# Chunk 2's loads in one run and its transposes behind all of them: a retention recurrence with a SwiGLU network on one core

## The chip, the core and the metric

The kernel runs on one core of a Trainium2 chip. The metric is the device time of one execution in microseconds (us). Five engines have in-order instruction queues of their own: TensorE (PE in the profile; PEld is its weight load), VectorE (DVE), ScalarE (ACT), GpSimd (POOL) and SyncE (SP, which here only issues DMAs). They meet through semaphores. DMAs that POOL issues appear in the profile as software DMAs on queue q0, those that SP issues as hardware DMAs on q1; TensorE's instructions come in on q8.

## The reference

Inputs are q, k, v of shape (4, 8, 768, 64): batch B, heads H, positions S, head width D. Each head h has a decay, and a recurrence over positions; its output, all heads side by side, goes through an RMS norm and a gated feed-forward network.

```python
gamma = 1.0 - 2.0 ** (-5.0 - np.arange(H))
for t in range(S):
    state = gamma[None, :, None, None] * state + np.einsum('bhd,bhe->bhde', k[:, :, t], v[:, :, t])
    y[:, :, t] = (1 / np.sqrt(D)) * np.einsum('bhd,bhde->bhe', q[:, :, t], state)
x = y.transpose(0, 2, 1, 3).reshape(B * S, H * D)          # 3072 x 512
xn = x / np.sqrt(np.mean(x * x, axis=-1, keepdims=True) + 1e-06) * rms_g
g = xn @ w_gate                                            # 512 x 1536
out = (g * sigmoid(g) * (xn @ w_val)) @ w_out              # 1536 x 512
```

The output is 3072 x 512 in float32.

## The kernel before

**Chunks and groups.** The 768 positions are cut into six chunks of 128. Within a chunk the recurrence is a masked product of q and k, applied to v (which carries the decay), plus q times the state from the chunks before. A chunk of all four batches is 512 tokens. The feed-forward network of chunk c is called group c here: twelve blocks of 128 hidden units in `gv` (gate and value products, eight or more matmuls each, then Silu on ScalarE and the multiplication `hT` on VectorE), and then `down`, once for each batch. The work of the recurrence for chunk c + 1 is placed between the steps of group c, so that TensorE has group c to work on while the other engines prepare the next chunk.

**Two ways to get q and k transposed.** Chunks 0 and 1 come as pairs of batches (`load_pair`, tiles q2b, k2b, v2f) and are transposed by TensorE. From chunk 2 on, `load` (line 103) issues three loads for one batch on POOL's queue: q and k, converted to bfloat16 on the way (qb, kb), and v in float32 (v_f). `t_dma` (line 486) then issues two DMA transposes on SP's queue, qb to qT and kb to kT. `vp` (line 480) on POOL multiplies v by its decay.

**The recurrence from chunk 2 on.** `a_pair(c, p)` makes the q-k products of the two batches of pair p on TensorE (line 499, tile a_ps, two PSUM banks a batch). `a_mask` multiplies them with the causal mask on VectorE (line 508). `values(c, p)` (line 518) adds three products: qT with the state, k with vp for the state's new term (bank kv_ps), and the masked products with vp. Then `y_out` (VectorE), `square` (ScalarE), `rstd` (POOL), `norm` (VectorE, tile xn) and `x_dma` (a DMA transpose on SP, xn to xnT, line 554) bring the pair's 256 tokens into the form that the next group's `gv` reads. `state_add` (VectorE, line 550) adds kv_ps to the float32 state, `state_cast` (POOL) makes its bfloat16 copy.

**What sets the order.** There is no scheduler: every engine executes its instructions in the order in which the program's text issues them (`manual_schedule`). For groups 1 and later, `run(steps, after)` issues step i of the list `steps` and then what the table `after` lists under i. Group 1 has sixteen steps: 0 to 11 are `gv`, of which 0 to 5 take the first 256 tokens (pair 0) and 6 to 11 the other 256, and 12 to 15 are `down` of batches 0 to 3. An entry of the table thus stands behind its step's matmuls in TensorE's queue, and behind that step's `hT` in VectorE's queue.

**Buffers.** A tile of the pools has a fixed number of buffers (8 of qb, kb, qT and kT, 6 of v_f), and an instruction that writes a buffer waits for its last reader. From group 1 on, PSUM's eight banks are two rotations: banks 0 to 3 serve the recurrence, 4 to 7 the network:

```python
        if i is None and split[0]:
            i = turn[ffn] % 4 + 4 * ffn
            turn[ffn] += 1
```

In the rotation of group 1, `values(2, 0)` takes banks 2 and 3 for y_ps and 0 for kv_ps, and `a_pair(2, 1)`, the next to ask, takes 1 and 2 for its first batch and 3 and 0 for its second.

**Where chunks 2 and 3 are loaded.** Before, the loads of chunk 2 are spread over the end of group 0, a batch at a time, with the transposes of a batch soon after: t_dma(2, 0) stands in SP's queue between the stores of group 0, and t_dma(2, 1) behind down(0, 3). Chunk 3 is loaded in steps 3 to 9 of group 1 and transposed in steps 8 to 12.

Of the kernel before, what the change touches and what calls it, by code (L numbers as in the profile page):

```python
# [16 lines left out]
def kernel(  # L17
# [11 lines left out]
    nc = tc.nc  # L29
# [58 lines left out]
    U = {}  # L88

# [13 lines left out]
    def load(c, b, names="qkv"):  # L103
        u = U.setdefault((c, b), {})
        for n in names:
            if n == "v":
                x = work.tile([128, H, D], F32, name="v_f", tag="v_f", bufs=6)
                nc.gpsimd.dma_start(out=x, in_=unit_v[n][c, b])  # L108
            else:
                x = work.tile([128, DM], BF16, name=n + "b", bufs=8)  # L110
                nc.gpsimd.dma_start(out=x.rearrange("p (h d) -> p h d", h=H), in_=unit_v[n][c, b])  # L111
            u[n] = x

# [372 lines left out]
    def t_dma(c, b):  # L486
        u = U[c, b]
        for n in "qk":
            t = work.tile([128, NHP, 128], BF16, name=n + "T", tag=n + "T", bufs=8)
            nc.sync.dma_start_transpose(out=t, in_=u[n])  # L490
# [98 lines left out]
    def down(c, b, n0=0, n1=NFF):  # L589
# [4 lines left out]
        if n1 == NFF:  # L594
            o_sb = work.tile([128, DM], F32, name="o_sb", bufs=3)
            nc.scalar.copy(o_sb, DP[b])  # L596
            store(nc.sync, c, b, slice(0, DM), o_sb)

# [103 lines left out]
    for n in "qk":  # L702
        load_pair(1, 1, n)
    vp_pair(1, 0)
    load_pair(1, 1, "v")
    load(2, 0)
# [25 lines left out]
    norm1(0)  # L732
    load(2, 1)
    vp_pair(1, 1)
    load(2, 2)
    t_dma(2, 0)
# [9 lines left out]
    load(2, 3)  # L746
    t_dma(2, 1)
    down(0, 3, 4, NFF)
    ap(1, 1, 0)
# [6 lines left out]
    def run(steps, after):  # L756
        for i, step in enumerate(steps):
            step()
# [3 lines left out]
    def L(f, *a):  # L762
# [8 lines left out]
        2: [L(begin, 2), L(norm, 1, 1, 0, 1), L(state_cast, 1), L(vp, 2, 0), L(vp, 2, 1), L(t_dma, 2, 2),  # L771
            L(t_dma, 2, 3)],
        3: [L(load, 3, 0)],
        4: [L(x_pe, 1, 1, 0), L(x_copy, 1, 1, 0, "v"), L(x_pe, 1, 1, 1), L(x_copy, 1, 1, 1, "a"), L(load, 3, 1)],
        5: [L(a_pair, 2, 0), L(a_mask, 2, 0, 0)],
        6: [L(a_mask, 2, 0, 1), L(a_mask, 2, 1, 0), L(vp, 2, 2), L(vp, 2, 3)],
        7: [L(a_mask, 2, 1, 1)],
        8: [L(values, 2, 0), L(load, 3, 2), L(t_dma, 3, 0), L(t_dma, 3, 1)],
        9: [L(y_out, 2, 0, 0), L(y_out, 2, 0, 1), L(state_add, 2, 0), L(load, 3, 3)],
        10: [L(a_pair, 2, 1), L(square, 2, 0, 0), L(a_mask, 2, 2, 0), L(a_mask, 2, 2, 1), L(state_cast, 0)],  # L780
        11: [L(square, 2, 0, 1), L(rstd, 2, 0), L(a_mask, 2, 3, 0), L(a_mask, 2, 3, 1), L(t_dma, 3, 2)],
        12: [L(values, 2, 1), L(norm, 2, 0, 0, 1), L(x_dma, 2, 0, 0), L(x_dma, 2, 0, 1), L(t_dma, 3, 3),
# [64 lines left out]
```

## Time and profile before

| | before |
|---|---|
| median of 13 runs | 245.06 us |
| lowest, highest run | 240.59, 249.2 us |
| profiled execution, its own time | 243.45 us |
| its span, first to last instruction | 241.5 us |
| mean granted TensorE clock | 0.985 |
| TensorE busy | 230.2 us, 95% of the span |
| POOL busy | 118.4 us, 49% |
| software DMA queue q0 | 52544 packets, 17.04 MB |
| hardware DMA queue q1 | 30224 packets, 12.72 MB |
| landing of a load of v_f, median of 16 | 8.2 us after its issue |
| landing of a kT transpose, median of 16 (least 2.4, most 10.2) | 7.2 us after its issue |

A DMA's row in a timeline is the time that the issuing engine spends on issuing it; when its data have landed is told apart, in the DMA view. In the busy rows a digit is the busy share of a fortieth of the span, in tenths. An idle time in square brackets is that of the engine just before the instruction, with what ended it; "issue" means that the profile shows nothing that it waited for. The clock column is the share of full speed that TensorE was granted. The DMA share sums the time of packets that overlap, so it can be above 1.

### The profile page before, as it was taken

Reading aid. Unit: us, or ns where it says so; the run is one execution under the profiler, and the core shown is the slowest. Engines: PE = TensorE matmul, PEld = TensorE weight load, DVE = VectorE, ACT = ScalarE, POOL = GpSimd, SP = SyncE. Lnnn points to the kernel's source line nnn. Section 1 sums busy time; section 2 is a strip of 40 time slices with the busy share of each in tenths; the row PEclk is TensorE's granted clock in tenths of the full one; section 3 lists DMA queues with packets and bytes.
Section 4 is the critical chain, followed back from the end, with each engine's and each line's share of the span. In section 5 each row is a group of like instructions: output and inputs, shape, how many; then the busy total and the mean of one; then the engine's idle time right before and its main releaser. Section 6 shows DMA issues by size and latency. Waiting matters only on the chain.

```text
span 241.5 us, 5543 instructions
## 1 busy us (share of the span) xinstructions
PE 230.2 (95%) x2281; PEld 138.3 (57%) x2281; DVE 127.5 (53%) x219; ACT 88.6 (37%) x178; POOL 118.4 (49%) x154
## 2 busy tenths in 40 slices
PE   7897999999889999999999999999999999999993
PEld 2465774455678875586454585454684444864443
DVE  3867433356756677826866437866245842234300
ACT  2866434208243243235323225313225242333221
POOL 8992948887959951990955901937001001000000
PEclk9978899999999999999999999999999999999999
DMA  9999999999999999999697993999520304200022
GB/s 109 157 175 190 160 172 148 177 205 167 142 197 155 155 184 128 189 145 204 49 153 173 115 169 131 101 121 174 134 86 0 46 0 124 96 0 0 0 90 87
DMA packets 83467, 30.25 MB, mean 125 GB/s; under 512 B 71602, under 2 KB 79026, under 8 KB 83443
## 3 DMA queue, kind: packets, MB, share of 16 engines
q0 software_dynamic: 52544, 17.04, 71.5%
q1 hardware_dynamic: 30224, 12.72, 29.0%
q8 instruction: 18, 0.29, 0.5%
q10 hardware_dynamic: 674, 0.14, 0.3%
q14 instruction: 7, 0.05, 0.1%
HBM read 28.32 MB, written 6.29 MB: 143 GB/s over the span
## 4 chain that ended last, share of the span: by engine, by line
PE 75%; DMA 7%; DVE 6%; POOL 5%; issue 3%; SPq 2%; ACT 1%; POOLq 0%; DVEq 0%; ACTq 0%
PE g_ps L571 23%; PE v_ps L571 23%; PE o_ps L593 20%; DMA v2f<-in_v_dram 3%; DMA kT<-kb 2%; DMA xnT<-xn 2%; DVE xn L468 2%; DVE am L508 2%; PE a_ps L499 1%; PE y_ps L544 1%; DVE hT L576 1%; SPq L490 1%; POOL q2b L99 1%; POOL k2b L99 1%; PE o_ps L605 1%
## 5 line engine op out<-in xcount | busy, mean ns | idle before, releaser
L576 DVE TENSOR_TENSOR hT<-sg,v_ps 128x512 bf16<-128x512 bf16 (+1 forms) x75 | 49.7, 664 | 76.1 <-PE v_ps L571 72.1
L571 PE MATMUL g_ps<-xnT,wg_b 128*128 128x256 bf16 (+1 forms) x424 | 75.5, 312 | 2.4 <-issue 1.9
L571 PE MATMUL v_ps<-xnT,wv_b 128*128 128x256 bf16 (+1 forms) x424 | 75.6, 313 | 0.0
L575 ACT ACTIVATE sg<-g_ps 128x512 bf16<-128x512 f32 (+1 forms) x75 | 43.4, 580 | 85.4 <-PE g_ps L571 85.4
L593 PE MATMUL o_ps<-wo_b,hT 128*128 128x512 bf16 x276 | 62.1, 379 | 0.1
L571 PEld LDWEIGHTS <-wv_b 128*128 128x128 bf16 x424 | 41.8, 99 | 21.4
L571 PEld LDWEIGHTS <-wg_b 128*128 128x128 bf16 x424 | 40.2, 98 | 23.0 <-issue 2.9
L593 PEld LDWEIGHTS <-hT 128*128 128x128 bf16 x276 | 26.4, 98 | 31.2 <-issue 0.4
L460 POOL TENSOR_SCALAR m<-ms 128x2 f32<-128x2 f32 x10 | 2.2, 219 | 69.3 <-ACT xsq L455 69.3
L596 ACT COPY o_sb<-o_ps 128x512 f32<-128x512 f32 x23 | 13.2, 580 | 33.8 <-PE o_ps L593 33.8
L468 DVE SCALAR_TENSOR_TENSOR xn<-x,rstd,g_bc 128x512 bf16<-128x512 f32 x18 | 18.5, 1054 | 8.5 <-POOL rstd L375 8.5
L508 DVE TENSOR_TENSOR am<-a_ps,causal 128x512 bf16<-128x512 f32 x32 | 20.8, 680 | 0.0
L482 POOL TENSOR_TENSOR vp<-v_f,vd_n 128x512 bf16<-128x512 f32 x16 | 20.1, 1278 | 0.0
L455 ACT ACTIVATE xsq<-x 128x512 bf16<-128x512 f32 x20 | 12.4, 623 | 13.5 <-DVE x L446 7.7
L111 POOL DMA_DIRECT2D qb<-in_q_dram x16 | 15.1, 942 | 0.0
L108 POOL DMA_DIRECT2D v_f<-in_v_dram x16 | 14.8, 924 | 0.0
L111 POOL DMA_DIRECT2D kb<-in_k_dram x16 | 14.4, 901 | 0.0
L220 PE MATMUL hot<-ones 128*128 128x512 bf16 x27 | 10.4, 521 | 1.4 <-DVE ones L143 1.4
L446 DVE TENSOR_TENSOR x<-y_ps,yd_n 128x512 f32<-128x512 f32 x16 | 10.8, 684 | 0.6 <-PE y_ps L544 0.6
L305 POOL TENSOR_TENSOR vp<-v2f,vd_p 128x1024 bf16<-128x1024 f32 x4 | 7.6, 1928 | 0.6 <-DMA v2f<-in_v_dram 0.6
L375 POOL TENSOR_TENSOR rstd<-m,mhalf 128x2 f32<-128x2 f32 x10 | 7.2, 718 | 0.8
L288 DVE TENSOR_TENSOR am<-a_ps,causal_p 128x512 bf16<-128x512 f32 x8 | 5.0, 684 | 2.6 <-PE a_ps L281 2.6
(99 smaller groups left out, 162.2 us busy)
## 6 DMA issues: line engine op xcount, KB each, us to landing
v_f<-in_v_dram POOLq DMA_DIRECT2D x16, 256.0 KB, 8.2
out_dram<-o_sb SPq DMA_DIRECT2D x15, 256.0 KB, 2.2
out_dram<-o_sb SPq DMA_DIRECT2D x17, 128.0 KB, 5.6
qb<-in_q_dram POOLq DMA_DIRECT2D x16, 128.0 KB, 6.5
kb<-in_k_dram POOLq DMA_DIRECT2D x16, 128.0 KB, 6.9
v2f<-in_v_dram POOLq DMA_DIRECT2D x7, 256.0 KB, 6.1
wo_b<-in_moe_w_out_dram POOLq DMA_DIRECT2D x3, 512.0 KB, 7.1
wg_b<-in_moe_w_gate_dram POOLq DMA_DIRECT2D x5, 256.0 KB, 6.7
```

The costliest lines, as they stand in the source:

```text
L108: nc.gpsimd.dma_start(out=x, in_=unit_v[n][c, b])
L111: nc.gpsimd.dma_start(out=x.rearrange("p (h d) -> p h d", h=H), in_=unit_v[n][c, b])
L446: nc.vector.tensor_tensor(out=x[:, :, :, i, :], in0=u["y"][i].rearrange("p (b a d) -> p b a d", b=2, a=NHP), in1=yd_n[:, c, i][:, None, :, ...
L455: nc.scalar.activation(xsq, u["x"][:, b], AF.Square, scale=1.0 / math.sqrt(DM), accum_out=u["ms_"][:, b:b + 1])
L468: nc.vector.scalar_tensor_tensor(out=u["xn"][b], in0=u["x"][:, b], scalar=u["rstd"][:, b:b + 1], in1=g_bc, op0=ALU.mult, op1=ALU.mult)
L482: nc.gpsimd.tensor_tensor(out=x, in0=U[c, b]["v"], in1=vd_n[:, c, :, None].to_broadcast([128, H, D]), op=ALU.mult)
L508: nc.vector.tensor_tensor(out=x, in0=u["a_ps"][i].rearrange("p (a t) -> p a t", a=NHP), in1=causal[:, None, :].to_broadcast([128, NHP, 128 ...
L571: nc.tensor.matmul(x[:, o:o + w], wt[:, s, n * 128:(n + 1) * 128], XT[c][:, s, t0:t1], start=s == 0, stop=s == KS - 1)
L575: nc.scalar.activation(sg[:, :m], ps[0][:, :m], AF.Silu)
L576: return nc.vector.tensor_tensor(out=HT[c][:, n0:n1, t0:t1], in0=sg[:, :m].rearrange("p (n t) -> p n t", t=w), in1=ps[1][:, :m].rearrange( ...
L593: nc.tensor.matmul(DP[b], HT[c][:, n, b * C:(b + 1) * C], wo_b[:, n, :], start=n == 0, stop=n == NFF - 1)
L596: nc.scalar.copy(o_sb, DP[b])
```

## The change

It has four parts.

1. The loads. v of pair (1, 1) is loaded ahead of its q and k, and POOL's product of it (`vp_pair(1, 1)`) comes up directly behind. q and k of batch (2, 0) are loaded where they were, and its v joins the run of loads of batches 1, 2 and 3, which POOL now issues with nothing between them.
2. The transposes of chunk 2. All eight are issued in one place, behind down(0, 3) and all stores of group 0 in SP's queue, and each waits for the last load of chunk 2 (`t_dma(2, b, "load")`, v of batch 3).
3. Chunk 3. Its first load waits for the `hT` of step 8 of group 1, and that of batch 2 for the o_sb copy of step 13 (`down` of batch 1), so that the loads of each half begin no earlier; the transposes of batches 0 and 1 come in step 10, those of 2 and 3 in step 15.
4. The recurrence in group 1. a_pair(2, 0) moves from step 5 to 7, values(2, 0) from 8 to 10, a_pair(2, 1) from 10 to 11, values(2, 1) from 12 to 13, a_pair(3, 0) from 14 to 15. state_add(2, 0) goes from behind y_out in step 9 to behind a_pair(2, 1) and the first of its masks in step 11.

The number of instructions on each engine, and what they compute, stay the same.

```diff
-    def load(c, b, names="qkv"):
+    def load(c, b, names="qkv", after=None):
...
+            if after is not None and after in MARK:
+                tc.add_manual_dep(i.ins, MARK[after].ins.name, SYNC_DEP, reason="transfer order")
             u[n] = x
+            MARK["load"] = i
...
-    def t_dma(c, b):
+    def t_dma(c, b, after=None):
...
-            nc.sync.dma_start_transpose(out=t, in_=u[n])
+            i = nc.sync.dma_start_transpose(out=t, in_=u[n])
+            if after is not None:
+                tc.add_manual_dep(i.ins, MARK[after].ins.name, SYNC_DEP, reason="transfer order")
...
-    for n in "qk":
-        load_pair(1, 1, n)
+    load_pair(1, 1, "v")
+    load_pair(1, 1, "q")
     vp_pair(1, 0)
-    load_pair(1, 1, "v")
-    load(2, 0)
+    load_pair(1, 1, "k")
+    load(2, 0, "qk")
+    vp_pair(1, 1)
...
     norm1(0)
+    load(2, 0, "v")
     load(2, 1)
-    vp_pair(1, 1)
     load(2, 2)
-    t_dma(2, 0)
+    load(2, 3)
...
-    load(2, 3)
-    t_dma(2, 1)
     down(0, 3, 4, NFF)
+    for b in range(B):
+        t_dma(2, b, "load")
...
-            step()
+            MARK[i] = step()
...
-        2: [L(begin, 2), L(norm, 1, 1, 0, 1), L(state_cast, 1), L(vp, 2, 0), L(vp, 2, 1), L(t_dma, 2, 2),
-            L(t_dma, 2, 3)],
-        3: [L(load, 3, 0)],
-        4: [L(x_pe, 1, 1, 0), L(x_copy, 1, 1, 0, "v"), L(x_pe, 1, 1, 1), L(x_copy, 1, 1, 1, "a"), L(load, 3, 1)],
-        5: [L(a_pair, 2, 0), L(a_mask, 2, 0, 0)],
-        6: [L(a_mask, 2, 0, 1), L(a_mask, 2, 1, 0), L(vp, 2, 2), L(vp, 2, 3)],
-        7: [L(a_mask, 2, 1, 1)],
-        8: [L(values, 2, 0), L(load, 3, 2), L(t_dma, 3, 0), L(t_dma, 3, 1)],
-        9: [L(y_out, 2, 0, 0), L(y_out, 2, 0, 1), L(state_add, 2, 0), L(load, 3, 3)],
-        10: [L(a_pair, 2, 1), L(square, 2, 0, 0), L(a_mask, 2, 2, 0), L(a_mask, 2, 2, 1), L(state_cast, 0)],
-        11: [L(square, 2, 0, 1), L(rstd, 2, 0), L(a_mask, 2, 3, 0), L(a_mask, 2, 3, 1), L(t_dma, 3, 2)],
-        12: [L(values, 2, 1), L(norm, 2, 0, 0, 1), L(x_dma, 2, 0, 0), L(x_dma, 2, 0, 1), L(t_dma, 3, 3),
-             L(y_out, 2, 1, 0), L(y_out, 2, 1, 1), L(state_add, 2, 1), L(square, 2, 1, 0), L(square, 2, 1, 1),
-             L(rstd, 2, 1), L(norm, 2, 1, 0, 1), L(x_dma, 2, 1, 0), L(x_dma, 2, 1, 1),
-             L(state_cast, 1), L(vp, 3, 0), L(vp, 3, 1)],
-        14: [L(a_pair, 3, 0), L(a_mask, 3, 0, 0, 1), L(a_mask, 3, 1, 0, 1)],
+        2: [L(begin, 2), L(norm, 1, 1, 0, 1), L(state_cast, 1), L(vp, 2, 0), L(vp, 2, 1)],
+        4: [L(x_pe, 1, 1, 0), L(x_copy, 1, 1, 0, "v"), L(x_pe, 1, 1, 1), L(x_copy, 1, 1, 1, "a")],
+        5: [L(vp, 2, 2), L(vp, 2, 3)],
+        7: [L(a_pair, 2, 0), L(a_mask, 2, 0, 0)],
+        8: [L(a_mask, 2, 0, 1), L(a_mask, 2, 1, 0), L(load, 3, 0, "qkv", 8)],
+        9: [L(a_mask, 2, 1, 1), L(load, 3, 1)],
+        10: [L(values, 2, 0), L(y_out, 2, 0, 0), L(y_out, 2, 0, 1), L(t_dma, 3, 0), L(t_dma, 3, 1)],
+        11: [L(a_pair, 2, 1), L(square, 2, 0, 0), L(square, 2, 0, 1), L(rstd, 2, 0), L(a_mask, 2, 2, 0),
+             L(state_add, 2, 0), L(state_cast, 0)],
+        12: [L(a_mask, 2, 2, 1), L(norm, 2, 0, 0, 1), L(x_dma, 2, 0, 0), L(x_dma, 2, 0, 1), L(a_mask, 2, 3, 0),
+             L(a_mask, 2, 3, 1)],
+        13: [L(values, 2, 1), L(load, 3, 2, "qkv", 13), L(y_out, 2, 1, 0), L(y_out, 2, 1, 1), L(square, 2, 1, 0),
+             L(square, 2, 1, 1), L(rstd, 2, 1), L(state_add, 2, 1), L(load, 3, 3), L(norm, 2, 1, 0, 1),
+             L(x_dma, 2, 1, 0), L(x_dma, 2, 1, 1), L(state_cast, 1), L(vp, 3, 0), L(vp, 3, 1)],
+        15: [L(a_pair, 3, 0), L(a_mask, 3, 0, 0, 1), L(a_mask, 3, 1, 0, 1), L(t_dma, 3, 2), L(t_dma, 3, 3)],
```

## The prediction

> **What bounds the kernel now.** I read the page first, then the busy time by stretches, then the timelines of TensorE, SP, POOL and VectorE from 40 us to 145 us, and last the DMA view in narrow windows, which gives one transfer's time from issue to landing.
>
> ```profile
> PE 230.2 (95%) x2281; PEld 138.3 (57%) x2281; DVE 127.5 (53%) x219; ACT 88.6 (37%) x178; POOL 118.4 (49%) x154
> ...
> DMA  9999999999999999999697993999520304200022
> ```
>
> TensorE is busy for 230.2 of 241.5 us, so all idle time that any change can remove is 11.3 us, and the kernel's start and its final tail hold most of it. The DMA row shows that the 16 engines are busy for the whole first half, where chunk 2 is fetched. The table by stretches (fields: stretch, length, then each engine's busy time, granted clock, DMA share, GB/s) finds what is left:
>
> ```profile
> 61.00:74.00 13.00, 11.05 (x189) 9.60 (x182) 9.12 (x14) 4.70 (x10) 10.57 (x12) 1.00 1.94 180
> 74.00:89.00 15.00, 14.65 (x192) 12.34 (x190) 9.92 (x17) 4.89 (x9) 13.50 (x16) 1.00 1.87 151
> 89.00:107.20 18.20, 18.01 (x201) 10.91 (x198) 11.83 (x17) 5.97 (x13) 11.44 (x14) 1.00 1.46 153
> ```
>
> From 61 to 107 us, the stretch of group 1, TensorE idles 1.95 + 0.35 + 0.19 us. That 2.5 us is the most the change can win there in this execution. The DMA share of 1.94 and 1.87 (packet time summed over overlapping packets) marks where loads and transposes share the engines. TensorE's timeline names the gaps:
>
> ```profile
> 64.65 0.83 PE L571 MATMUL g_ps<-xnT,wg_b 128*128 128x256 bf16 x6
> 67.43 0.39 PE L571 MATMUL g_ps<-xnT,wg_b 128*128 128x256 bf16 x2 [1.95 <-issue]
> ...
> 76.06 0.62 PE L499 MATMUL a_ps<-qT,kT 64*128 64x128 bf16 x16
> ...
> 87.70 0.38 PE L499 MATMUL a_ps<-qT,kT 64*128 64x128 bf16 x7 [0.33 <-DVE st_f L550]
> ...
> 107.21 1.05 PE L571 MATMUL g_ps<-xnT,wg_b 128*128 128x256 bf16 x8 [0.20 <-DMA xnT<-xn]
> ```
>
> The 1.95 us gap waits for no semaphore. In 64 to 67 us the DMA view has one packet of 0.02 MB on the instruction queue (q8), and the bandwidth falls to 0 to 14 GB/s for over a microsecond, so I read it as TensorE out of instructions behind a clogged DMA system (argued, not shown). The product of the first pair (76.06) does not wait for its transposes: the last of them, kT of batch 1, was issued at 65.04 and landed after 9.4 us, at 74.4. The SP queue and the DMA view give the transfers:
>
> ```profile
> 74.72 1.19 SPq L490 DMA_TRANSPOSE qT<-qb  x1
> 78.01 1.19 SPq L490 DMA_TRANSPOSE kT<-kb  x1
> ```
>
> ```profile
> 66.46 0.95 POOL L108 DMA_DIRECT2D v_f<-in_v_dram  x1
> ```
>
> ```profile
> v_f<-in_v_dram POOLq DMA_DIRECT2D x1, 256.0 KB, 12.2
> ```
>
> ```profile
> kT<-kb SPq DMA_TRANSPOSE x1, 9.4
> ```
>
> ```profile
> kT<-kb SPq DMA_TRANSPOSE x1, 2.4
> ```
>
> The last load of chunk 2 was issued at 66.46 and took 12.2 us, to 78.7. A transpose among loads takes 9.4 us; the same transpose alone (issued at 132.17) takes 2.4 us and SP issues one each 1.3 us (130.87, 132.17, 133.47).
>
> **What the Trainium skill says.** "DMA: Bandwidth & Descriptors", section "Issuing engines are not separate DMA queues": DMAs from POOL and SP run on the same 16 engines and interleave. The 9.4 against 2.4 us agree. The same page, section "Two DMAs through the same engine are not ordered", says that order needs a wait of the issuing engine on the earlier DMA's semaphore; that is what the change adds on SP, so everything behind it in SP's queue waits too. "TensorE: Matmul & The Clock Gate", section "What's actually happening": the clock halves after about one idle window of 3.4 us. The trace agrees in part: after 19.40 to 22.81 (1.74 us busy) the clock is 0.50 until 26.22, but after 63.77 to 67.18 (1.71 us busy) it stays 1.00. No page prices an instruction fetch that comes late.
>
> **The change part by part.** Times are on the clock of the profiled execution.
>
> *Loads.* v of (1,1) goes ahead of its q and k, its 1.94 us product on POOL (60.19) moves to about 52.6, into POOL's idle 2.4 us before 55.94, and v of (2,0) moves from 52.6 to 57.5. From 57.5 POOL then issues ten loads of chunk 2 at 0.91 us each (median of the rows), to 66.6: no gain on POOL. k of (1,1) is now issued at 49.4 to 50.8; v in that slot landed at 55.6 and 57.1, and its transposes start at 57.9. Cover 0.8 us, cost nothing; if it fails, a few tenths.
> When does the last load land? Without transposes beside them, six loads issued from 103.03 to 107.51 landed from 106.9 (3.9 us) to 114.4 (6.9 us): 1.5 us each, stores among them. The first here is issued at 57.5 and lands after 4.0 us as before, at 61.5; nine more at 1.45 us: **74.5**. From below: POOL's last issue 65.7 plus 3.4 us (the quickest load), 69.1. From above: the 78.7 of before.
>
> *Transposes.* All eight now wait for that landing; before, the first was issued at 59.36. SP issues back to back and, with chunk 3 held back, nothing contends: kT of batch 1 is the fourth, issued at 74.6 + 3 x 1.3 = 78.5, landed at **81.0**. The eighth lands by 74.6 + 7 x 1.3 + 2.5 = 86.2, or 88 once chunk 3 loads beside it. Ahead of them SP issues all eight half stores, and behind them the stores and transposes of chunk 3 come later than before, where nothing waits at that time.
>
> *First products.* a_pair(2,0) moves from behind step 5 to behind step 7. In before, step 7 ends at 80.12 with the product's 0.55 inside it, so without stalls TensorE is there at 79.57; if the 1.95 us gap goes, at 77.6. It then waits until 81.0 either way, and ends at 81.3 (its second half, 0.28, follows kT). Against 80.12: **+1.2 us**. The gap that goes is turned into this wait. The two gv steps of delay bought 3.5 us; the transposes come 6.6 us later (81.0 against 74.4).
>
> *Second products and the state.* a_pair(2,1) takes four PSUM banks of the attention four: the rotation gives it the bank of kv, which state_add(2,0) has to free. Before, state_add stood right behind y_out, a step ahead of the product (wait 0.33). Now values(2,0) is at step 10, a_pair(2,1) at step 11, and the order puts VectorE's state_add behind hT of step 11 and behind the first mask of the same a_pair. From the end of step 11 on TensorE: 0.1 + 0.6 hT + 0.65 mask + 0.65 state_add = 2.0 us until batch 3's second matmul may start, against 0.28 us of matmuls of batch 2. The pair so takes 2.45 us; before it took 1.27 (86.74 to 88.01). **+1.2 us**. Bounds: 0 if VectorE were to finish early, which its order excludes, and 2 if a mask waits.
>
> *Clock.* Without the 1.95 us gap TensorE stands from 77.6 to 81.0. A halved window costs 1.7 us (half of 3.41). By the two windows above it may come or not, and it depends on where the window begins: bounds 0 and 1.7, I take half, **+0.9 us**.
>
> *Into group 2.* values(2,1) moves from step 12 to 13, one down (2.63 us) later. Before, its y_ps ended at 93.8 and xnT landed at 107.2, with 2.4 us lost in SP's queue behind t_dma(3,3). After, on a base shifted by 2.3: y_ps 98.7, y_out 100, squares 101.4, rstd 102.4, norms 103.5 and 104.7, landing 4.5 us later at 109.2; TensorE needs it at 107.0 + 2.3 = 109.3. **+0.3**, bounds 0 and 1.5, since chunk 3 loads beside it. kT of (3,3), now moved behind step 15, lands about 116 for a need at 117; nothing. The q and k wait of TensorE for chunk 5 (0.2 us at 167) shifts along.
>
> Sum: 1.2 + 1.2 + 0.9 + 0.3 = **+3.6 us**. The profiled execution took 243.45 us (its span 241.5 and 1.95 around it), so 247.05. The median of the runs is 245.06, which is 1.6 above. If those 1.6 us are gaps of the same kind in the same stretch, the new wait swallows them; if elsewhere, they stay. I take half: **247.9 us**.
>
> **Rivals.** (a) *Slower still*: the loads end at 77 (the clog of 65 us comes without transposes too), +2.5, and xnT of the second pair is late by 0.6 more: 251.0. For it: the 12.2 us of the last load. Against it: without transposes no load took over 8.6 us in 38 to 57 us. (b) *Nothing changes*: the loads run at 1.3 us each (118 to 120 us has 1548 load packets, of 1024 a load), the last lands at 73.2, kT at 79.7; the first product ends 0.1 us ahead of before, state_add costs 1.2, the clock holds: +1.1, so 245.3 by the same step to the median. (c) *Faster*: the runs spread from 240.6 to 249.2, and if this spread is loads and transposes colliding, a stage with the two kept apart runs each time as the best of before, 240.6, plus 1.2 for state_add and 0.4: 242.2. One mechanism, the collision in 59 to 79 us; it decides if the last load lands before 71.1, for then kT (6.5 us later) is there when TensorE arrives at 77.6; that needs 1.07 us a load. For it: the 1.95 us gap and the 9.4 us transposes. Against it: the measured 1.5.
>
> **How the numbers follow.** Forecast 0.45 (own range 246 to 250), (a) 0.20, (b) 0.20, (c) 0.15. 1%, about what a measurement of this kernel can tell from no change, is 242.6 and 247.5. Faster: nearly all of (c), 0.15. Within 1%: (b) and the lower third of the forecast, less a little, 0.30. Slower: 0.55. The range 243.0 to 251.5 leaves out most of (c) and the upper half of (a), some 0.2.
>
> **What would show each step.** Right: the first kT of chunk 2 issued right after the last v lands, near 74.5; a_ps of L505 waiting for DMA kT near 78 to 81; a second wait of 1.5 us or more for st_f near 90; no gap at 65; a clock of 0.50 in one window after 81 or not at all. Wrong: chunk 2's last load landing before 71, or TensorE without a wait at the first product; then the forecast falls to (b) or (c).

## The result, and the profile after

The changed kernel takes 251.86 us (median of 11 runs, 247.63 to 255.59); the kernel before, run beside it, 246.76 us (median of 48, 239.83 to 255.21). By the medians that is +5.1 us. The ratio is 1.0314, 95% interval [1.0258, 1.037]; ratios here rest on the executions of each kernel near its own fastest, medians on all of them. The profiled execution took 250.05 us, with a span of 248.1 us and a mean granted clock of 0.986. The forecast was 247.9 us.

The page of the changed kernel, the row of busy times and the DMA row:

```profile
PE 230.8 (93%) x2281; PEld 138.0 (56%) x2281; DVE 126.5 (51%) x219; ACT 88.6 (36%) x178; POOL 117.7 (47%) x154
...
DMA  8999999998965499999999599399540213300022
```

TensorE is as busy as before (230.8 against 230.2 us) and the span is 6.6 us longer: the change added idle time and no work. TensorE's timeline names the idle times (the last field: idle before the row, and what ended it):

```profile
53.27 0.20 PE L425 MATMUL y_ps<-vp,am 64*128 64x64 bf16 x2 [1.74 <-issue]
81.03 0.40 PE L505 MATMUL a_ps<-qT,kT 64*128 64x128 bf16 x8 [2.06 <-DMA kT<-kb]
93.52 0.38 PE L505 MATMUL a_ps<-qT,kT 64*128 64x128 bf16 x7 [1.66 <-DVE st_f L556]
114.17 1.03 PE L577 MATMUL g_ps<-xnT,wg_b 128*128 128x256 bf16 x8 [3.09 <-DMA xnT<-xn]
```

Before, the corresponding rows had 0.39 us of issue at 53.56, no wait at the first product, 0.33 us for st_f and 0.20 us for xnT; its 1.95 us of issue at 67.43 has no counterpart after. The row at 53 us before:

```profile
53.56 0.21 PE L421 MATMUL y_ps<-vp,am 64*128 64x64 bf16 x2 [0.39 <-issue]
```

The table by stretches of the changed kernel shows the stretches of the forecast first, and then windows of 3.41 us, the length of a stretch at half clock in these two profiles:

```profile
61.00:74.00 13.00, 13.00 (x205) 11.05 (x203) 10.54 (x18) 6.20 (x13) 10.24 (x12) 1.00 1.28 166
74.00:89.00 15.00, 12.94 (x139) 10.43 (x136) 6.37 (x11) 3.60 (x7) 4.42 (x6) 0.89 0.55 80
...
78.20:81.61 3.41, 1.34 (x24) 0.82 (x22) 1.29 (x2) 0.20 (x1) 0.00 (x0) 1.00 0.57 82
81.61:85.03 3.42, 3.42 (x19) 2.44 (x17) 0.17 (x1) 0.60 (x1) 0.00 (x0) 0.50 0.57 110
...
50.90:54.31 3.41, 1.67 (x69) 1.24 (x68) 0.93 (x3) 0.10 (x1) 2.33 (x2) 1.00 1.93 158
54.31:57.72 3.41, 3.41 (x10) 1.19 (x9) 2.15 (x4) 2.50 (x7) 2.06 (x5) 0.50 0.51 58
```

The change does what it says: between 61 and 74 us TensorE no longer idles, and from 74 to 89 us the DMA share falls from 1.87 to 0.55, since until 85.85 us no load stands beside the transposes. But TensorE idles for 2.06 us in that stretch, and the window behind the wait (81.61 to 85.03) runs at half clock, as does the one behind the gap at 53 us (54.31 to 57.72). A window at half clock (a "half window" below) costs 1.7 us, half of its length. Before had two of them too, at the start (12.57 and 22.81), so the mean clocks of the two profiled executions are alike.

The transfers behind this, from the timelines of POOL and SP and from the DMA view (us from issue to landing, in narrow windows around each issue):

```profile
65.12 0.98 POOL L109 DMA_DIRECT2D v_f<-in_v_dram  x1
```

```profile
77.49 1.21 SPq L494 DMA_TRANSPOSE kT<-kb  x1
...
105.12 2.58 SPq L560 DMA_TRANSPOSE xnT<-xn  x2
```

```profile
v_f<-in_v_dram POOLq DMA_DIRECT2D x1, 256.0 KB, 8.2
```

```profile
kT<-kb SPq DMA_TRANSPOSE x1, 3.5
```

```profile
xnT<-xn SPq DMA_TRANSPOSE x1, 7.6
```

The last load of chunk 2 landed at 65.12 + 8.2 = 73.3 and the fourth transpose at 77.49 + 3.5 = 81.0. The second xnT of pair 1 was issued at 106.40 (the second of the two at 105.12) and landed at 114.0, where it took 4.6 us before.

### The profile page after: what moved, and what is told of

Same layout as the page of the kernel before. It is cut to its first block, busy times and chain, and to the rows that moved or that the text cites. A ratio compares the mean times of both kernels' runs of the same rounds, so it can differ in the third digit from the quotient of the medians.

```text
span 248.1 us, 5543 instructions
## 1 busy us (share of the span) xinstructions
PE 230.8 (93%) x2281; PEld 138.0 (56%) x2281; DVE 126.5 (51%) x219; ACT 88.6 (36%) x178; POOL 117.7 (47%) x154
## 4 chain that ended last, share of the span: by engine, by line
PE 82%; DMA 7%; POOL 5%; DVE 2%; issue 2%; ACT 1%; DVEq 0%; POOLq 0%; ACTq 0%
PE o_ps L599 25%; PE g_ps L577 24%; PE v_ps L577 24%; DMA xnT<-xn 3%; DMA v2f<-in_v_dram 3%; PE y_ps L550 2%; PE a_ps L505 2%; DMA kT<-kb 1%; POOL q2b L100 1%; POOL k2b L100 1%; PE o_ps L612 1%; PE y_ps L534 1%; PE kv_ps L543 1%; PE x_ps L399 1%; POOL wg_b L83 1%
## 5 line engine op out<-in xcount | busy, mean ns | idle before, releaser
L599 PE MATMUL o_ps<-wo_b,hT 128*128 128x512 bf16 x276 | 63.4, 387 | 0.0
L472 DVE SCALAR_TENSOR_TENSOR xn<-x,rstd,g_bc 128x512 bf16<-128x512 f32 x18 | 17.4, 994 | 8.5 <-POOL rstd L379 8.5
L486 POOL TENSOR_TENSOR vp<-v_f,vd_n 128x512 bf16<-128x512 f32 x16 | 19.2, 1217 | 3.3 <-DMA v_f<-in_v_dram 3.3
L450 DVE TENSOR_TENSOR x<-y_ps,yd_n 128x512 f32<-128x512 f32 x16 | 10.8, 684 | 4.4 <-PE y_ps L550 4.4
L224 PE MATMUL hot<-ones 128*128 128x512 bf16 x27 | 9.7, 492 | 1.4 <-DVE ones L147 1.4
L505 PE MATMUL a_ps<-qT,kT 64*128 64x128 bf16 x128 | 5.3, 217 | 3.7 <-DMA kT<-kb 2.1
```

The lines of the kernel that those rows point to most:

```text
L450: nc.vector.tensor_tensor(out=x[:, :, :, i, :], in0=u["y"][i].rearrange("p (b a d) -> p b a d", b=2, a=NHP), in1=yd_n[:, c, i][:, None, :, ...
L472: nc.vector.scalar_tensor_tensor(out=u["xn"][b], in0=u["x"][:, b], scalar=u["rstd"][:, b:b + 1], in1=g_bc, op0=ALU.mult, op1=ALU.mult)
L486: nc.gpsimd.tensor_tensor(out=x, in0=U[c, b]["v"], in1=vd_n[:, c, :, None].to_broadcast([128, H, D]), op=ALU.mult)
L599: nc.tensor.matmul(DP[b], HT[c][:, n, b * C:(b + 1) * C], wo_b[:, n, :], start=n == 0, stop=n == NFF - 1)
```

## The experiments

All edits are against the changed kernel unless they say "against before". Times are medians; "its before" is the kernel before, measured beside it. The theory at the start (A in the expectations) was that the loss is three new waits, and that the largest, for xnT, comes from chunk 3's loads beside its transposes.

### The parts one by one

**Part 4 alone (e7).** Against before, only the rows of the table that place the products:

```diff
-        5: [L(a_pair, 2, 0), L(a_mask, 2, 0, 0)],
+        7: [L(a_pair, 2, 0), L(a_mask, 2, 0, 0)],
...
-        8: [L(values, 2, 0), L(load, 3, 2), L(t_dma, 3, 0), L(t_dma, 3, 1)],
+        10: [L(values, 2, 0), L(y_out, 2, 0, 0), L(y_out, 2, 0, 1)],
```

> The kernel before with only the fourth part of the change: the recurrence's work of group 1 (a_pair, a_mask, values, y_out, state_add, norm, x_dma) in the steps of the changed kernel, loads and transposes issued in the places of the kernel before, none of them with an added wait. If the placement costs what the forecast said, TensorE waits 1.5 us for st_f, none at the first product, under 1 us for xnT, and the kernel takes 1 to 2 us more than before (ratio 1.004 to 1.008). If most of the loss is the placement, the wait for xnT is 2 to 3 us here too and the ratio is 1.015 or more. If most of the loss is the order of the transfers, the ratio is below 1.008.

248.37 us (13 runs), its before 246.74; ratio 0.9943 [0.9846, 1.004]. The medians say +1.6, the interval neither gain nor loss. In its profile the wait for st_f is 1.66 us, as in the changed kernel, and there is no wait for kT or xnT. So what the placement costs alone is not shown.

**Parts 1, 2 and 3 without 4 (f4).** The products go back to before's steps. The second half of chunk 3's loads goes with them, to step 12 in place of 13, as it also does in g2 and h1:

```diff
-        7: [L(a_pair, 2, 0), L(a_mask, 2, 0, 0)],
+        5: [L(a_pair, 2, 0), L(a_mask, 2, 0, 0)],
```

> The changed kernel's transfers (loads of chunk 2 in one run, its transposes behind all of them, chunk 3 held back to step 8 and step 12, its last transposes behind step 14) with the recurrence's work in the steps of the kernel before. Theory (the order of the transfers is the loss, and the later placement only softens it): TensorE waits 4.5 to 6 us at the first product, which stands at 75 us while kT lands at 81, the wait for st_f is under 0.5 us, the wait for xnT stays at 2 to 3 us, and the kernel takes 251 to 255 us. Rival (the placement is the loss): 249 us or less.

249.46 us, its before 246.25 (+3.2); ratio 1.0243 [1.0164, 1.0321]. TensorE waits twice for kT (1.98 and 2.21 us), st_f costs 0.33 and xnT 0.38. The time lies between the two that were expected. The later placement is not what keeps the loss of the transfers small: without it the kernel is, if anything, faster. The xnT transposes of pair 1 took 6.1 us here too, but they landed at 111.7 and were read at 113.1; the 0.38 us are for pair 0's.

**Parts 1 and 2 alone (g3).** Against before, chunk 2's loads in one run and its gated transposes; chunk 3 and the products stay:

```diff
+    load(2, 3)
...
-    load(2, 3)
-    t_dma(2, 1)
     down(0, 3, 4, NFF)
+    for b in range(B):
+        t_dma(2, b, "load")
```

> The kernel before with the other part of the transfers' change alone: chunk 2's loads in one run, its transposes behind all of them, each waiting for the last load; chunk 3's loads and transposes and the steps of the recurrence are those of the kernel before. If the order within chunk 2 is the larger part of the loss, TensorE waits 4 us or more for kT at the two first products, chunk 3's loads (from 72 us on) run beside the transposes and make them longer than 2.5 us, and the ratio is 1.015 to 1.03. If holding chunk 3 back is the larger part, the ratio is under 1.01.

252.95 us, its before 247.52 (+5.4); ratio 1.0293 [1.0222, 1.0363]. By the medians the whole size of the loss is there already. TensorE's timeline of this kernel:

```profile
80.28 0.61 PE L505 MATMUL a_ps<-qT,kT 64*128 64x128 bf16 x8 [7.50 <-DMA kT<-kb]
84.15 0.61 PE L505 MATMUL a_ps<-qT,kT 64*128 64x128 bf16 x8 [3.26 <-DMA kT<-kb]
```

With the product at its old step and chunk 3's loads beside the transposes (6.9 us for the first kT, 8.0 for the second, against 2.4 to 3.5 in the changed kernel), 10.8 us of waiting come together. No wait for xnT is left.

**Part 3 alone (g2, and again as h1).** Against before, chunk 3 held back and nothing else:

```diff
-        3: [L(load, 3, 0)],
...
-        8: [L(values, 2, 0), L(load, 3, 2), L(t_dma, 3, 0), L(t_dma, 3, 1)],
+        8: [L(values, 2, 0), L(load, 3, 0, "qkv", 8)],
```

> The kernel before with one part of the change: chunk 3 is held back (loads of batches 0 and 1 behind steps 8 and 9, the first waiting for step 8; those of 2 and 3 behind step 12, the first waiting for it; its transposes in steps 10 and 14). Chunk 2's transfers and the steps of the recurrence are those of the kernel before. If holding chunk 3 back is the larger part of the loss, the ratio is 1.012 to 1.02, and the xnT transposes of pair 1 take over 5 us. If it costs nothing by itself, the ratio is under 1.006: chunk 2's transposes then have the engines for themselves from 67 us on and land before 80.

244.63 us (19 runs), its before 247.52 (40 runs); ratio 0.9948 [0.9862, 1.0034].

> The kernel of before with nothing but chunk 3 held back, a second time, for a narrower interval. Theory (the order within chunk 2 is the whole loss, and holding chunk 3 back is worth something, because chunk 2's transposes then have no loads beside them): median 1 to 2.5 us below before, 244 to 246, ratio 0.99 to 0.995. Rival (the gain of the first measurement was chance): the median equals that of before within 0.5 us.

242.20 us (6 runs), its before 246.18; ratio 0.9912 [0.9773, 1.0051]. Both medians lie below before (-2.9 and -4.0 us) and both intervals touch 1: likely the best version here, not shown to be. TensorE's timeline of g2, and the DMA view at the issue of kT of batch 1 (65.71):

```profile
66.36 0.39 PE L577 MATMUL g_ps<-xnT,wg_b 128*128 128x256 bf16 x2 [2.75 <-issue]
102.84 1.03 PE L577 MATMUL g_ps<-xnT,wg_b 128*128 128x256 bf16 x8 [1.67 <-DMA xnT<-xn]
```

```profile
kT<-kb SPq DMA_TRANSPOSE x1, 8.2
```

A wait for xnT is there (1.67 us; 2.55 in h1): it comes with part 3, though here it is pair 0's second transpose (issued at 95.89, landed at 102.7) that is late and not, as in the changed kernel, pair 1's. But kT of batch 1, slow as it is among loads, has landed at 73.9, 7 us earlier than in the changed kernel, and no product of chunk 2 waits for a transpose.

**Parts 3 and 4 without 1 and 2 (h2).** The changed kernel with chunk 2's loads and transposes put back:

```diff
-    load(2, 3)
+    t_dma(2, 0)
...
+    load(2, 3)
+    t_dma(2, 1)
     down(0, 3, 4, NFF)
-    for b in range(B):
-        t_dma(2, b, "load")
```

> The changed kernel with parts 1 and 2 alone undone: chunk 2 is loaded and transposed as before, chunk 3 is held back and the products are placed as in the change. Theory: with parts 1 and 2 gone the loss of 5 us is gone, 244 to 247 us; no wait of the first product for kT of over 1 us; the wait for st_f of about 1.7 us stays, so it is 0 to 1.5 us above the kernel with chunk 3 held back alone. Rival (the loss needs the held back chunk 3 or the later placement as well): 248.5 us or more.

244.78 us, its before 246.18 (-1.4); ratio 1.0072 [0.9973, 1.0172]. The loss is gone. TensorE's timeline:

```profile
63.74 0.39 PE L577 MATMUL g_ps<-xnT,wg_b 128*128 128x256 bf16 x2 [0.55 <-issue]
86.91 0.38 PE L505 MATMUL a_ps<-qT,kT 64*128 64x128 bf16 x7 [1.66 <-DVE st_f L556]
108.34 1.44 PE L577 MATMUL g_ps<-xnT,wg_b 128*128 128x256 bf16 x8 [3.86 <-DMA xnT<-xn]
```

Its wait for xnT is the longest of all, and the kernel is no slower than before. The wait begins at 108.34 - 3.86 = 104.5, while the changed kernel gets there at 114.17 - 3.09 = 111.1 and before at 107.0. Of the 6.6 us between h2 and the changed kernel some 3.4 are the two half windows that the latter has had by then and h2 has not. So most of what is lost in the changed kernel is lost ahead of this wait.

**Before once more (e5).** The kernel before, unchanged, for a second profile.

> The kernel before, unchanged, for a second profile of it. Theory A (the 1.95 us gap at 65 us, which the forecast counted as removed by the change, belongs to the collision of loads and transposes): it appears again near 65 us, 1.5 us or more, and the gap near 53 us stays under 0.5 us. Rival B (TensorE's instructions come late somewhere in the stretch of small matmuls in every execution, in a place that varies): the gap stands at 53 us, as in the changed kernel (1.74 us), or in both places with other sizes; then the change removed nothing there.

247.13 us in that one execution. TensorE's timeline:

```profile
74.95 0.40 PE L499 MATMUL a_ps<-qT,kT 64*128 64x128 bf16 x8 [2.44 <-DMA kT<-kb]
90.32 0.40 PE L499 MATMUL a_ps<-qT,kT 64*128 64x128 bf16 x8 [4.51 <-DMA kT<-kb]
```

The forecast rested on an execution in which neither product waited. It was a lucky one: of the five profiles in which chunk 2 is loaded as before and chunk 3 is not held back (before, e5, e7, f2, g4), three have such waits, with 7.0, 1.5 and 4.9 us in sum; of the three in which chunk 3 is held back (g2, h1, h2), none.

### The waits that the change makes

**The gate (e3).** The added wait for the last load goes; each transpose waits for its own load only:

```diff
-        t_dma(2, b, "load")
+        t_dma(2, b)
```

> The changed kernel, but each transpose of chunk 2 waits only for its own load and not for the last load of the chunk. Its place in SP's queue stays. Theory A (the wait at the first q-k product is the added order and nothing else): kT of batch 1 lands by 76, TensorE's 2.06 us wait for it goes, the half-clock window behind it (81.6 to 85.0 us, 1.7 us) goes too, and the kernel is 3 to 4 us faster than the changed one. Rival B (transposes among loads cost the loads and the instruction fetch as much): the last load of chunk 2 lands near 78 instead of 73.3, a gap of 1 to 2 us with no cause shown appears between 60 and 70 us, and the gain is under 2 us.

250.90 us, its before 246.16; ratio 1.0191 [0.9873, 1.0509], too wide for a verdict. The profile tells more: kT of batch 1 was issued 10 us earlier, at 67.70, and the DMA view there has

```profile
kT<-kb SPq DMA_TRANSPOSE x1, 12.4
```

so kT landed at 80.1, 0.9 us earlier than with the gate, and TensorE waits for kT 0.78 and then 2.08 us. The loads pay as well: the last of chunk 2 landed at 79.9, against 73.3 with the gate. So taking the gate away wins almost nothing, as rival B had it, though its gap between 60 and 70 us did not come. What else makes the transposes late was not taken apart. Two things fit: their place behind all stores of group 0 on SP (first issue 63.09; 57.51 in h2), and the closed run of loads beside them. Before, batch 1's transposes do not stand behind all of down(0, 3), as the section on the kernel has it: SP issues them at 63.66 and 65.04, ahead of the last two half stores at 67.33.

**Filling the wait (e4, e8).** As filler, TensorE multiplies a constant into a bank that nothing reads, nine times ahead of the first product, and in e8 also 13 times ahead of the wait for xnT:

```diff
-        7: [L(a_pair, 2, 0), L(a_mask, 2, 0, 0)],
+        7: [L(heat, 9, 0), L(a_pair, 2, 0), L(a_mask, 2, 0, 0)],
```

> The changed kernel with nine more matmuls of 128x512 on constants (1.9 us at full clock) in front of a_pair(2,0), where TensorE waits for its transposes anyway; their result is not used. Theory A (the wait costs twice, once as a wait and once as a half-clock window behind it): the wait becomes work, the clock stays 1.00 from 78 to 86 us, and the kernel is 1.2 to 1.7 us faster than the changed one. Rival B (the half clock there has another cause or comes anyway): the clock of 0.50 stays and the time is the same or up to 0.5 us longer.

250.88 us (one of six runs, of 395.75, stands apart), its before 246.16; ratio 1.0237 [1.0043, 1.0431]: no half window after the product, but others at 22.2, 56.3 and 114.3.

> The changed kernel with nine matmuls of 128x512 on constants in front of a_pair(2,0) and thirteen (2.8 us at full clock) behind values(3,0), in front of the gv that waits for xnT; their results are not used. Theory A (each wait costs again as a half-clock window): TensorE's granted clock over the span rises from a median of 0.983 to 0.990 or more, as in the kernel before, and the kernel is 1 to 2.5 us faster than the changed one. Rival B (the half-clock windows are those of the start and of the gap near 53 us): the clock stays near 0.983 and the time within 1 us.

248.93 us, its before 246.74; ratio 1.017 [1.0053, 1.0288]. The median granted clock rises from 0.983 to 0.998. With (1 - clock) x span as the time lost to the clock, the changed kernel loses 4.5 us a run and e8 1.4 (means of all runs), while the rest of the span is 245.0 and 245.3 us. So some 3 us can be won back by keeping TensorE from idling. But not all of the 3 are the change's: the kernel before loses 3.0 us to the clock itself (mean of the 18 runs beside e8), so that the change added some 1.5. "TensorE: Matmul & The Clock Gate" of the Trainium skill, section "What's actually happening", has a halving follow an idle window; 1.34 us busy of 3.41 were idle enough here (the window from 78.20, above).

**state_add (e2, f2).** It goes back directly behind y_out:

```diff
-        10: [L(values, 2, 0), L(y_out, 2, 0, 0), L(y_out, 2, 0, 1), L(t_dma, 3, 0), L(t_dma, 3, 1)],
+        10: [L(values, 2, 0), L(y_out, 2, 0, 0), L(y_out, 2, 0, 1), L(state_add, 2, 0), L(t_dma, 3, 0), L(t_dma, 3, 1)],
```

> The changed kernel, but state_add(2,0) is back directly behind y_out(2,0), in step 10. Theory (the kv bank that a_pair(2,1) needs is freed late because of where state_add stands in VectorE's queue): TensorE's wait for st_f falls from 1.66 to 0.4 us or less, and the kernel is 1.0 to 1.3 us faster than the changed one. Rival (VectorE is the limit there, or the next wait takes its place): the wait falls, but the wait for xnT grows by as much, and the time stays within 0.5 us.

249.81 us, +3.7 on its before; ratio 1.0289 [1.019, 1.0388]. The wait for st_f is gone and kT's (2.80 us) stands. TensorE also waits 2.79 us for xnT, but for pair 0's second transpose, issued at 100.32 and landed at 107.0; pair 1's, landed at 113.2, is there before it is read. By medians 1.5 us are won, about the wait; the intervals overlap.

> The kernel before with the later placement of the recurrence's work in group 1 (the fourth part of the change) but state_add(2,0) directly behind y_out; no wait is added. If the placement is harmless once the kv bank is freed in time, TensorE's wait for st_f (1.66 us with the placement as changed) falls under 0.4 us, and the ratio to before is 0.985 to 0.998. If the later values step costs at the entry to group 2, a wait for xnT of 1 us or more is seen and the ratio is 1.0 or more.

f2 is e7 with the same edit: 246.16 us, its before 246.25; ratio 1.0155 [1.0112, 1.0199]. The profile has 1.46 us for kT and 2.35 for xnT where the 1.66 went. The wait for xnT and the ratio are those of the second branch, a cost at the entry to group 2, but the medians are level, so whether it costs anything stays open. This xnT, pair 1's, was not slow but late: issued at 103.67, it landed after 3.9 us.

### Where the wait for xnT comes from

**Loads of chunk 3 ahead of it (e1).**

```diff
-        9: [L(a_mask, 2, 1, 1), L(load, 3, 1)],
+        9: [L(a_mask, 2, 1, 1), L(load, 3, 1), L(load, 3, 2), L(load, 3, 3)],
```

> The changed kernel, but the loads of chunk 3's batches 2 and 3 follow those of batch 1 in step 9 and no longer wait for step 13, so that they have landed before the xnT transposes of pair 1 are issued (105.1 and 106.4 us in the changed kernel's profile, landing after 5.7 and 7.6 us). Theory A (those transposes are late because the last six loads of chunk 3 share the DMA engines with them): they land in under 5 us, TensorE's wait for xnT falls from 3.09 to under 0.7 us, and the kernel is 2 to 3 us faster than the changed one. Rival B (the chain is late because values(2,1) stands one step later, 2.6 us): the wait stays above 2 us and the time moves by less than 1 us.

256.49 us, its before 246.16; ratio 1.0419 [1.0205, 1.0634]. xnT of pair 1 now lands after 2.5 and 3.8 us and is no longer waited for; TensorE's timeline and the DMA view at 114.2 show what came instead:

```profile
124.21 0.56 PE L505 MATMUL a_ps<-qT,kT 64*128 64x128 bf16 x8 [4.18 <-DMA kT<-kb]
127.73 0.61 PE L505 MATMUL a_ps<-qT,kT 64*128 64x128 bf16 x8 [2.96 <-DMA kT<-kb]
```

```profile
kT<-kb SPq DMA_TRANSPOSE x1, 10.0
```

The transposes of chunk 3 now stand beside chunk 4's loads.

**Loads of chunk 3 behind it (g1).** The loads of batches 2 and 3 wait for the last xnT transpose of chunk 2 and are issued behind it:

```diff
-        13: [L(values, 2, 1), L(load, 3, 2, "qkv", 13), L(y_out, 2, 1, 0), L(y_out, 2, 1, 1), L(square, 2, 1, 0),
+        13: [L(values, 2, 1), L(y_out, 2, 1, 0), L(y_out, 2, 1, 1), L(square, 2, 1, 0),
...
+             L(x_dma, 2, 1, 0), L(x_dma, 2, 1, 1), L(state_cast, 1), L(vp, 3, 0), L(vp, 3, 1), L(load, 3, 2, "qkv", "x"), L(load, 3, 3)],
```

> The changed kernel, but the loads of chunk 3's batches 2 and 3 wait until the last xnT transpose of chunk 2 has landed. Theory A (those loads beside the xnT transposes of pair 1 are what makes them late): both transposes land in under 4 us, TensorE's wait for xnT (3.09 us) falls under 0.5 us; the wait comes back later, 1 to 3 us for kT of chunk 3's pair 1 in group 2, since its loads are now 4 to 6 us later. Rival B (the chain or SP's queue makes them late): the transposes are issued at the same times and still land after 5 us or more.

256.06 us (4 runs), its before 247.52; ratio 1.0424 [1.0346, 1.0502]. The DMA view at the issue of the second xnT, 107.2, and the timeline:

```profile
xnT<-xn SPq DMA_TRANSPOSE x1, 3.1
```

```profile
122.50 0.40 PE L505 MATMUL a_ps<-qT,kT 64*128 64x128 bf16 x8 [4.21 <-DMA kT<-kb]
```

With no load beside it xnT takes 3.1 us and nothing waits for it: that its 7.6 us in the changed kernel come from chunk 3's loads is shown, by moving them ahead (e1) and behind (g1). Both times the wait comes back, larger, at the next transposes.

**The pair earlier (e6).** With e2's edit, values(2, 1) and what follows it move from step 13 to 12:

```diff
-        13: [L(values, 2, 1), L(load, 3, 2, "qkv", 13), L(y_out, 2, 1, 0), L(y_out, 2, 1, 1), L(square, 2, 1, 0),
+        12: [L(values, 2, 1), L(norm, 2, 0, 0, 1), L(x_dma, 2, 0, 0), L(x_dma, 2, 0, 1), L(load, 3, 2, "qkv", 12),
```

> The changed kernel with state_add(2,0) behind y_out and values(2,1), with all that follows from it up to the xnT transposes and the second half of chunk 3's loads, in step 12 instead of 13. Theory B (one step later is what makes xnT late): the chain starts 2.6 us earlier, TensorE's wait for xnT falls from 3.09 us to 0.5 us or less, the wait for st_f goes, and the kernel is 3 to 4.5 us faster than the changed one (247 to 249 us). Theory A (the loads of chunk 3 beside these transposes make them late wherever they stand): the loads move along with the chain, so the transposes still take 5 to 8 us, and the wait falls by the 2.6 us at most, to 0.5 us, if the landing times stay; if the wait stays above 1 us, A alone explains it.

251.84 us, its before 246.74; ratio 1.0343 [1.0256, 1.043]. The xnT transposes of pair 1 were issued at 103.7 and 105.1 and landed after 7.9 and 6.7 us, about as slowly as in the changed kernel, the later one at 111.8; but they are read only at 113.8, and TensorE no longer waits for them. It waits for pair 0's second transpose, issued at 102.17 and landed at 108.9, since the loads moved along and now stand beside pair 0. SP's and TensorE's timelines:

```profile
100.75 5.62 SPq L560 DMA_TRANSPOSE xnT<-xn  x4
```

```profile
109.06 1.03 PE L577 MATMUL g_ps<-xnT,wg_b 128*128 128x256 bf16 x8 [2.69 <-DMA xnT<-xn]
```

The loads make the transposes slow wherever they meet (theory A); the placement decides which of them TensorE has to wait for. With before's steps the wait is 0.38 us (f4), 1.67 (g2) or 2.55 (h1), as pair 0's second transpose lands after 5.4, 6.8 or 7.7 us.

**Chunk 4 held back too (f1; f3 with nine fillers).** e1 and e2 together, and chunk 4's first load waits for the last transpose of chunk 3:

```diff
-                2: [L(y_out, d, 0, 0)] + [L(load, d + 1, 0)] * more,
+                2: [L(y_out, d, 0, 0)] + [L(load, d + 1, 0, "qkv", "t" if c == 2 else None)] * more,
```

> The changed kernel with state_add(2,0) behind y_out, all of chunk 3's loads in steps 8 and 9, and the first load of chunk 4 waiting for the last transpose of chunk 3, so that neither the xnT transposes of pair 1 nor those of chunk 3 run beside loads. Theory A (every transpose that runs beside loads is late, and this alone made xnT late): the xnT transposes of pair 1 land in under 5 us, TensorE's waits for xnT, for st_f and for kT of chunk 3 are each under 0.8 us, the wait of 2 us at the first product stays, and the kernel is 4 to 5 us faster than the changed one, 246 to 248 us, level with the kernel before. Rival (the transfers have only so much room in this stretch, and what is freed at one place is missing at the next): a new wait of 2 us or more appears in group 2, for kT or behind rstd of chunk 3, which now stands behind the held-back loads in POOL's queue, and the time stays above 249 us.

253.34 us, its before 246.25; ratio 1.0433 [1.0353, 1.0512]. No wait for xnT or for kT of chunk 3, but TensorE's timeline has

```profile
80.36 0.40 PE L506 MATMUL a_ps<-qT,kT 64*128 64x128 bf16 x8 [3.38 <-DMA kT<-kb]
97.99 0.44 PE L544 MATMUL kv_ps<-vp,kb 128*64 128x64 bf16 x16 [2.66 <-DVE am L515]
```

The twelve loads in a row on POOL hold up rstd(2, 0); norm(2, 0) and the masks behind it on VectorE wait, and with them the second product of values.

> The kernel of the run with chunk 4 held back (state_add behind y_out, chunk 3's loads in steps 8 and 9, chunk 4's first load behind chunk 3's last transpose) with nine matmuls of 128x512 on constants in front of a_pair(2,0); their result is not used. If the wait at the first product costs a half-clock window too, the granted clock rises by 0.003 or more against that run and the time falls by 1 to 1.7 us, to 245 to 247 us. If not, the two are within 0.5 us.

254.20 us, its before 246.25; ratio 1.0411 [1.0313, 1.051]. The filler shortens the first wait to 0.68 us, and kv_ps waits 3.42 instead. Nothing won.

### Filler in the kernel before (g4)

Six fillers behind group 0's last work, against before:

```diff
+    heat(6, 7)
```

> The kernel before with six matmuls of 128x512 on constants (1.3 us at full clock) in front of y0(1,0), where TensorE waits 0.7 to 1.6 us near 20 us for the cast of v in the profiles; their result is not used. If a filled wait keeps the clock there as it does in group 1, the granted clock's mean rises by 0.002 to 0.004 and the kernel is 0.3 to 1.0 us faster than before (ratio 0.996 to 0.999). If the half-clock windows of the start have another cause, the ratio is 1.000 to 1.003.

245.36 us (22 runs), its before 247.52; ratio 1.0024 [0.9935, 1.0114]: no clear effect. That filler would help the kernel before as it helps e8 is not shown.

## Why the prediction was wrong

The direction held, and so did the first two of the four terms of the sum; the rise was taken too small. The step that failed is the last term, "Into group 2".

*Loads and transposes: right.* Last landing forecast 74.5, measured 73.3; kT of batch 1 forecast 81.0, measured 81.0. That the last figure is met so closely is luck: the loads landed 1.3 us apart, the pace of rival (b) and not the 1.5 of the forecast, and the fourth transpose took 3.5 us and not 2.5. The 1.5 was read from six loads said to be without transposes, but two xnT transposes stood beside them until 107.2. Rival (b) had the loads right (73.2), but not its kT of 79.7: the first transpose was issued at 73.47, the fourth 4.0 us later, and that took 3.5. Rival (c) fell, as its condition said.

*First product: right.* TensorE waits until 81.03, forecast 81.0. The 1.95 us gap of 67.43 did go. In its place stands one of 1.74 us at 53.27, not foreseen, which the wait for kT swallows.

*Second product and st_f: right.* The wait is 1.66 against 0.33 us, +1.3 where +1.2 was forecast. VectorE's timeline has the order that the forecast worked out, hT, mask, st_f:

```profile
91.58 0.69 DVE L582 TENSOR_TENSOR hT<-sg,v_ps 128x512 bf16<-128x512 bf16 x1 [0.56 <-PE v_ps L577]
92.19 0.68 DVE L514 TENSOR_TENSOR am<-a_ps,causal 128x512 bf16<-128x512 f32 x1
92.79 0.68 DVE L556 TENSOR_TENSOR st_f<-st_f,kv_ps 128x512 f32<-128x512 f32 x1
```

*Clock: too small.* Half of 1.7 was taken; the window at 81.61 had the whole 1.7. When TensorE reaches the wait for xnT (111.08 after, 107.01 before), the changed kernel is 4.07 us late, where the first three terms gave 3.3; the 0.8 between them is this term. Over all runs the time lost to the clock rose from 3.0 us (mean of the 18 runs beside e8) to 4.5, so the direction at least is no chance of one execution.

*"Into group 2": the term that failed.* Forecast +0.3 with a bound of 1.5, measured 3.09 - 0.20 = +2.9. The second x_dma was worked out for 104.7 and issued at 106.40, 1.7 us later; TensorE's need was put at 109.3 and came at 111.1, 1.8 later: these cancel. What is left is the landing, set at 4.5 us, the figure of before; part 3 puts the last six loads of chunk 3 about it, of which four are in flight when it is issued, and it took 7.6. The same text reads transposes among loads at 9.4 us and prices part 3 with "since chunk 3 loads beside it" at a bound of 1.5: the number was on the page and was not used. e1 and g1 show that these loads are what made it slow. This is 2.6 of the 3.0 us that the profiled execution (250.05) lies above the forecast for it (247.05).

*The base.* The forecast measured every term against an execution of before without a wait for kT, so it could give part 3 no gain. The runs divide the loss otherwise than the sum does. By medians against the before measured beside each, parts 1 and 2 cost 5.4 us alone (g3), 3.2 + 2.9 = 6.1 on top of part 3 (f4 against g2) and 5.1 + 1.4 = 6.5 on top of parts 3 and 4 (the change against h2). Part 4 costs 1.6 alone (e7, though its ratio of 0.9943 shows none), 2.6 on top of part 3 (h2 against h1) and 1.9 on top of the rest (the change against f4), near its wait for st_f. Part 3 gives 2.9 to 4.0 (g2, h1), its wait for xnT included. About 6 + 2 - 3 makes the measured 5.1; this is an estimate, since the intervals of the single runs are 3 to 7 us wide, and only the share of parts 1 and 2 stands clear of them. The forecast had some 2.1 for parts 1, 2 and their clock, 1.2 for part 4 and 0.3 for part 3: two errors of opposite sign, of which the first is the larger. That the sum came within 4 us of the result is in part luck.

*What stays open.* First, the gap without a visible cause: all twelve profiles with chunk 2's loads in one run have 1.2 to 2.3 us of it near 53 us and none over 0.3 near 65; the eight others have at most 0.7 near 53 and from nothing to 2.75 near 65. A late fetch of instructions fits, and the traces say more than the forecast used: each of the 24 such gaps of over 0.3 us between 15 and 240 us, in all 20 profiles, ends 1.4 to 1.9 us after a packet of 16 KB on the instruction queue q8 is through. In the changed kernel the packet ahead of the gap at 53 us started between 50.3 and 50.4 and took 1.38 us (86.3% of 16 engines in a window of 0.1 us); before, the one between 50.9 and 51.0 took 0.89. The DMA views of the two windows, changed kernel first:

```profile
q8 instruction: 1, 0.02, 86.3%
...
q8 instruction: 1, 0.02, 55.8%
```

No run moved these packets, so it stays argued. Second, whether the run of loads (part 1) or the late place of the transposes (part 2) makes the larger loss: apart from the gate, they were only tried together. And third, whether part 3 alone beats the kernel before: two medians say so, no interval does.

## What to carry over

A DMA transpose that stands alone is quick, but making it stand alone means to wait for the last load, and that wait can be longer than the time won: here the fourth transpose went from 9.4 to 3.5 us and still landed at 81.0 us, where before it had landed at 74.5. Nor is it enough to take the wait away again: behind all stores and beside the run of loads it landed at 80.1 (e3). If transfers are to be separated, the ones to hold back are those that nobody needs yet (part 3, no loss by two medians), not those that the next product waits for (parts 1 and 2, 5.4 to 6.5 us by medians). When a transfer is moved, price the landing of everything that it now stands beside, from rows of the same trace with the same neighbours, and take more than one profile of the kernel before as the base.

## What the runs showed of the hardware

- A transpose of 128 KB with no load in flight took 2.4 to 4.2 us, median 2.5 (268 of them in the 20 profiles); with loads in flight from its issue to its landing, 3.2 to 13.0 us, median 6.9 (283 of them). The slowing is mutual: in e3 the kb load of chunk 2's last batch, issued at 64.16 with transposes beside it, took 15.0 us; in the changed kernel, where the loads stand in the same order, it was issued at 64.26 with only loads and stores about it and took 8.5.
- A wait of TensorE can cost twice: behind the 2.06 us at 81.03 in the changed kernel stands a window at half clock that costs 1.7 us more. It need not: the 3.09 us at 114.17 in the same profile, and the 2.08 us at 80.11 in e3, have none behind them. Filling two waits with unused products brought the time lost to the clock from 4.5 to 1.4 us a run, with the rest of the span unchanged.
- The gap with no releaser stands near 53 us, 1.2 to 2.3 us long, wherever chunk 2's loads are issued in one run; with the other order it is at most 0.7 us there and up to 2.75 near 65. TensorE's program around it is the same in all these kernels, and each such gap ends 1.4 to 1.9 us after a 16 KB packet on q8, which fits q8 as the queue that brings TensorE's instructions.
